# A TensorE loop for the products with V, and a fence that places the loads of the next step

## Chip, core and metric

The kernel runs on one core of a Trainium2 chip. The metric is the device time of one execution in microseconds (us), lower is better. The engines are PE (TensorE, with PEld for its weight loads), DVE (VectorE), ACT (ScalarE), POOL (GpSimd) and SP (SyncE, which here only issues DMAs). Each engine works through its own stream of instructions in order; engines wait for each other through semaphores.

## What is computed

One decode step of a transformer block: layer norm, attention of one query token per batch element over a cache of 8192 keys, output projection, and a gated MLP. What fills the time is the attention over the cache:

```python
B, Sq, D = 2, 1, 512
Hq, Hkv, Sk, Dh = 32, 32, 8192, 128          # k_cache, v_cache: (B, Hkv, Sk, Dh) in bf16
q = (layernorm(x) @ wq)                      # one row per batch element and head
scores = einsum("bhqd,bhkd->bhqk", q, k_cache) * Dh ** -0.5
p = softmax(scores)
o = einsum("bhqk,bhkd->bhqd", p, v_cache)
h = x + o.reshape(B, Sq, Hq * Dh) @ wo       # then a gated MLP of 512 x 1376
```

The two caches are 268 MB, each byte of which is used once.

## The kernel before

**Tiles and steps.** Four heads of one batch element make a step. Their keys are one tile of 8 MB (128 partitions x 32768 bf16), their values another. Fifteen whole steps (`steps[0]` to `steps[14]`, with `Q = LASTQ = 14`) and two half steps of two heads each cover all 64 heads. Three buffers of one tile each (`bufs`) are used in rotation in the order K0, V0, K1, V1, K2 and so on: V of step i+1 goes where K of step i was, K of step i+2 goes where V of step i was. So a load waits for the last reader of the tile that it replaces.

**One step** (the loop `for i in range(Q)` at the end of the kernel's attention part):

1. `scores_pe` (L343 to L370): PE transposes the last 24 of the 256 key columns of a partition (32 in step 0), ACT copies them back, PE multiplies them with the query.
2. `products` (L378) and `scores` (L396 to L402): DVE multiplies the other 232 columns with the query and adds them up by halving, about 33 us. This reads K for the last time.
3. `largest_of_own` and `place_own` (L413 to L423): DVE and ACT make the exponentials and lay them out as PE weights in `pgq`, with one group of 16 weight columns for each of 64 products.
4. `values` (L449): 64 products on PE, each a weight load of 128x16 and a matmul over 512 columns of V, all summed in one PSUM tile `pv_ps`. This reads V for the last time. Then ACT copies `pv_ps` to `pv` (L454).

In steps after 3, 7 and 11 the first eight products stand ahead of a small sum (`ahead = 8`).

**Order.** `tc.manual_schedule()` keeps every engine's instructions in the order in which the text issues them. Loads are issued by SP (`load_tile`, L168), in text order, each after its own waits. V of step i+1 is issued in the text after `scores` of step i and waits for DVE's last sum L398; K of step i+2 is issued after `values` of step i and waits for the last of its 64 products.

Of the kernel before, what the change touches and what calls it, by code (L numbers as in the profile page):

```python
# [7 lines left out]
ACT = mybir.ActivationFunctionType  # L8
# [15 lines left out]
def kernel(  # L24
# [13 lines left out]
    nc = tc.nc  # L38
    P = nc.NUM_PARTITIONS
    B, Sq, D = A_x.shape  # L40
    _, Hkv, Sk, Dh = A_k_cache.shape
# [13 lines left out]
    HALF = TILE // 2  # L55
    TPC = 8
    VG = 4


    NPE = 32  # L60
# [37 lines left out]
    qpair = consts.tile([P, 2, Dh], bf16)  # L98
    pgq = consts.tile([P, TILE // Dh // VG, NH, VG], bf16)
    pgp = consts.tile([P, 2, HALF // Dh // VG, 2, VG], bf16)  # L100
    pv = consts.tile([P, VG * Dh], f32)
    pick = consts.tile([P, VG, 4, NH], f32)
    zc = consts.tile([P, B, NQ, NH], f32)
# [56 lines left out]
    steps = [Step(i) for i in range(LASTQ + 3)]  # L160
    Q = LASTQ

    def load_tile(cache, s, dst, pieces=1):
        h = NH * s.g + (0 if s.quad else 2 * s.k)
        n = s.nt * Dh
        w = n // pieces
        for k in range(pieces):
            nc.sync.dma_start(  # L168
                out=dst[:, k * w:(k + 1) * w], in_=_dram(cache, (s.b * Hkv + h) * Sk * Dh + k * w, [[n, P], [1, w]]),
            )  # L170
# [16 lines left out]
        nc.vector.reciprocal(out=rstd, in_=rstd)  # L187
        nc.vector.tensor_tensor(out=dst_bkc, in0=dev, in1=_free(rstd, 0, [[1, B], [0, KC]]), op=ALU.mult)

    with tc.manual_schedule():  # L190

        for b, k, n in ((0, 0, KC), (1, 0, KC)):
            nc.scalar.dma_start(
                out=xr[b:b + 1, k * P:(k + n) * P], in_=_dram(A_x, b * D + k * P, [[D, 1], [1, n * P]]),
# [10 lines left out]
            out=nscale, in_=nscale, compare_op=ALU.not_equal, fill=-SCALE,  # L205
# [5 lines left out]
            out=ident_f, in_=ident_f, compare_op=ALU.not_equal, fill=1.0,  # L211
# [4 lines left out]
            out=sel, in_=sel, compare_op=ALU.not_equal, fill=1.0,  # L216
# [9 lines left out]
            out=pick, in_=pick, compare_op=ALU.not_equal, fill=1.0,  # L226
# [24 lines left out]
        for g0 in range(0, NQ, 4):  # L251
            for n0 in range(NH * g0 * Dh, NH * (g0 + 4) * Dh, 4 * Dh):
                q_ps = ps2.tile([B, 4 * Dh], f32, tag="o")
                for c in range(KC):
                    nc.tensor.matmul(  # L255
                        out=q_ps, lhsT=xn[:, c, :], rhs=wq_sb[:, c, n0:n0 + 4 * Dh], start=(c == 0), stop=(c == KC - 1),
                    )
                nc.vector.tensor_copy(qrow[:, n0:n0 + 4 * Dh], q_ps)  # L258
            for b in range(B):
                r_ps = ps2.tile([P, 4, Dh], f32, tag="tp")  # L260
                for j in range(NH):
                    nc.tensor.matmul(
                        out=r_ps[j * (P // NH):(j + 1) * (P // NH)], lhsT=sel[:, b, 0:P // NH],
                        rhs=_free(qrow, (NH * g0 + j) * Dh, [[NH * Dh, 4], [1, Dh]]), start=True, stop=True,
# [4 lines left out]
        for j in range(2):  # L269
            nc.tensor.matmul(  # L270
                out=r_ps[j * (P // 2):(j + 1) * (P // 2)], lhsT=sel[:, B - 1, :],
                rhs=_free(qrow, (Hq - NH + j) * Dh, [[2 * Dh, 2], [1, Dh]]), start=True, stop=True,
            )
        nc.scalar.activation(out=qpair, in_=r_ps, func=ACT.Copy)
        for b in range(B):
# [3 lines left out]
            nc.vector.tensor_copy(  # L279
                qTs[:, b].rearrange("p (g j) -> p g j", j=NH), _free(qT_ps, 0, [[P, NQ], [P // NH, NH]]),  # L280
            )
        load_tile(A_k_cache, steps[1], steps[1].kt)

        nc.gpsimd.tensor_copy(
            qzp[:, :, 6:8], qTs[:, B - 1, Hq - NH:Hq].rearrange("p (k j) -> p k j", j=2),
        )
# [42 lines left out]
        def scores_pe(s, between=lambda: None):  # L329


            U = s.npe // 4
            nh, nv = s.nh, s.nv
            row_ps = ps.tile([nh * U, 4 * P], f32, tag="row")

            def times_q(c0):
                for k in range(0, TPC, 4):
                    u = (c0 + k) // 4
                    if s.quad:
                        z = qz[:, QZ - NH - NH * u:QZ - NH - NH * u + NH * U]  # L340
                    else:
                        z = qzp[:, s.k, 6 - 2 * u:6 - 2 * u + 2 * U]
                    nc.tensor.matmul(  # L343
                        out=row_ps, lhsT=z, rhs=s.kt[:, (nv + c0 + k) * Dh:(nv + c0 + k + 4) * Dh],
                        start=(u == 0), stop=(u == U - 1),
                    )

            for c0 in range(0, s.npe, TPC):
                t_ps = ps2.tile([P, TPC, P], bf16, tag="tp")
                for k in range(TPC):  # L350
                    t = nv + c0 + k
                    nc.tensor.transpose(t_ps[:, k, :], s.kt[:, t * Dh:(t + 1) * Dh], ident)  # L352
                nc.scalar.activation(  # L353
                    out=s.kt[:, (nv + c0) * Dh:(nv + c0 + TPC) * Dh], in_=t_ps.rearrange("p t s -> p (t s)"), func=ACT.Copy,
                )
                between()
                if c0:
                    times_q(c0 - TPC)
            times_q(s.npe - TPC)
            rows = s.kt[0:nh * U, nv * Dh:nv * Dh + 8 * P].bitcast(f32)  # L360
            nc.scalar.activation(out=rows, in_=row_ps, func=ACT.Copy)  # L361
            between()
            sc_ps = ps.tile([P, 4, U, nh], f32, tag="row", name="sc_ps")
            for t in range(4):
                nc.tensor.transpose(  # L365
                    sc_ps[:, t].rearrange("p u j -> p (u j)"), rows[:, t * P:(t + 1) * P], ident_f[0:nh * U, 0:nh * U],
                )
            for j in range(nh):
                r = s.rows(j)
                nc.scalar.activation(  # L370
                    out=scols[s.i][r, nv:s.nt].rearrange("p (u t) -> p t u", t=4), in_=sc_ps[r, :, :, j], func=ACT.Copy,
                )
# [67 lines left out]

        pv_ps = {}

        def values(s, u0, u1):

            r = slice(32 * (s.g % 4), 32 * (s.g % 4) + s.nh * VG)
            if u0 == 0:
                pv_ps[s.i] = ps2.tile([P, VG * Dh], f32, tag="o", name="pv_ps")
            for u in range(u0, u1):
                nc.tensor.matmul(  # L449
                    out=pv_ps[s.i][r, :], lhsT=s.pg[:, u].rearrange("p j t -> p (j t)"),  # L450
                    rhs=s.vt[:, u * VG * Dh:(u + 1) * VG * Dh], start=(u == 0), stop=(u == s.nt // VG - 1),
                )
            if u1 == s.nt // VG:
                nc.scalar.activation(out=pv[r, :], in_=pv_ps[s.i][r, :], func=ACT.Copy)  # L454

        def diagonals(i):

# [54 lines left out]
        for i in range(Q):  # L512
            s = steps[i]
            scols[i] = small.tile([P, s.nt], f32, tag="scol", name="scol")
            scores_pe(s)
            place_q(steps[i + 1])
            products(s)
            if i - 2 in groups:
                shares(i - 2)
                normalise(i - 2)  # L520
            if i == Q - 1:
                lay_rows(0, [spread(0, b) for b in range(B)], scalar=True)
            scores(s)
            if i == Q - 2:
                load_tile(A_k_cache, steps[Q], steps[Q].kt)
            else:
                load_tile(A_v_cache, steps[i + 1], steps[i + 1].vt)
            if i == Q - 1:
                scores_pe(steps[Q])
            largest_of_own(s)  # L530
            if i == Q - 1:
                products(steps[Q], 0, NEXT)
            place_own(s)
            half = s.nt // VG // 2
            ahead = 8 if i - 1 in groups else 0
            if ahead:
                own_sums(i - 1)
                values(s, 0, ahead)
                sums(i - 1)
            values(s, ahead, half)  # L540
            if i == Q - 1:
                load_tile(A_k_cache, steps[Q + 1], steps[Q + 1].kt)
            values(s, half, 2 * half)
            if i in groups:
                diagonals(i)
            if i + 2 < Q:
                load_tile(A_k_cache, steps[i + 2], steps[i + 2].kt)
            elif i == Q - 2:
                load_tile(A_v_cache, steps[Q - 1], steps[Q - 1].vt)
            else:  # L550
                load_tile(A_k_cache, steps[Q + 2], steps[Q + 2].kt)


        s, p0, p1 = steps[Q:]
# [16 lines left out]
        at = [0, 0]  # L571
# [28 lines left out]
        turns = iter((first, second, third))  # L600
# [3 lines left out]
        for w, src in ((0, B_W_gate), (1, B_W_up)):  # L604
            nc.sync.dma_start(
                out=wgu[:, w].rearrange("p c f -> p (c f)"), in_=_dram(src, 0, [[KC * F, P], [1, KC * F]]),
# [4 lines left out]
        f0, n = FSETS[-2]  # L611
        for d0 in range(0, D, D // 2):
            nc.sync.dma_start(
                out=wd_sb[:, f0 // P:f0 // P + n, d0:d0 + D // 2],
                in_=_dram(B_W_down, f0 * D + d0, [[n * D, P], [D, n], [1, D // 2]]),
# [9 lines left out]
            out=z2_ps, lhsT=ones, rhs=_free(zc, ((B - 1) * NQ + groups[Q][1]) * NH, [[1, nb]]), start=True, stop=True,  # L625
# [11 lines left out]
            out=parts3, in0=ident[0:PARTS, HI:HI + B], in1=ident[0:PARTS, LOW:LOW + B], op=ALU.add,  # L637
# [3 lines left out]
        half = p1.nt // 2  # L641
# [53 lines left out]
        for c in range(KC):  # L695
            nc.tensor.transpose(hT_ps[:, c, :], hb[:, c], ident)
        nc.scalar.activation(
            out=hrow.rearrange("q (p c) -> q p c", c=KC), in_=hT_ps.rearrange("q c p -> q p c"), func=ACT.Copy,
# [3 lines left out]
            out=shift, in0=_free(g_ps, ONE, [[ONE + 1, FC], [0, B]]), in1=_free(mean, 0, [[0, FC], [1, B]]), op=ALU.mult,  # L702
# [3 lines left out]
            out=gate, in_=_free(g_ps, 0, [[ONE + 1, FC], [1, B], [B, 2]]), axis=AXIS.X, op=ALU.add,  # L706
# [7 lines left out]
            out=gate, in0=gate, scalar=0.0, in1=_free(rvar, 0, [[0, FC], [1, B]]), op0=ALU.max, op1=ALU.mult,  # L714
# [63 lines left out]
```

## Time and profile before

| | |
|---|---|
| median of 3 runs | 659.2 us (659.19 to 659.33) |
| the profiled execution | 658.71 us, span 656.9 us |
| DVE busy | 557.1 us (85% of the span) |
| PE busy | 348.8 us (53%), granted clock 0.761 on average |
| ACT busy | 123.6 us (19%) |
| HBM read | 281.09 MB, 428 GB/s over the span |
| products with V (PE L449) | 960 of 128x512, 239.7 us busy |

"Span" is the time from the first to the last instruction in the trace; what the execution's own time has above it (1.8 us) lies around it. Busy shares are shares of the span. The chain of waits in such a profile is followed back from the last instruction: at each step to what released it.

### The profile page before, as it was taken

Reading aid. Unit: us, or ns where it says so; the run is one execution under the profiler, and the core shown is the slowest. Engines: PE = TensorE matmul, PEld = TensorE weight load, DVE = VectorE, ACT = ScalarE, POOL = GpSimd, SP = SyncE. Lnnn points to the kernel's source line nnn. Section 1 sums busy time; section 2 is a strip of 40 time slices with the busy share of each in tenths; the row PEclk is TensorE's granted clock in tenths of the full one; section 3 lists DMA queues with packets and bytes.
Section 4 is the critical chain, followed back from the end, with each engine's and each line's share of the span. In section 5 each row is a group of like instructions: output and inputs, shape, how many; then the busy total and the mean of one; then the engine's idle time right before and its main releaser. Section 6 shows DMA issues by size and latency. Waiting matters only on the chain.

```text
span 656.9 us, 5097 instructions
## 1 busy us (share of the span) xinstructions
PE 348.8 (53%) x2116; PEld 157.9 (24%) x2116; DVE 557.1 (85%) x248; ACT 123.6 (19%) x337; POOL 9.1 (1%) x37
## 2 busy tenths in 40 slices
PE   2530924709175380926538092562909458291997
PEld 1210311304022130312214031220403224130456
DVE  1399697988979799897979989797997969999982
ACT  1130030300203030030302103030210304201870
POOL 3000000000000000000000000000000000000020
PEclk9875876958778695877959588695957869576895
DMA  9999999999999999999999999999999999999997
GB/s 383 447 444 443 391 448 439 447 443 397 447 439 432 447 408 447 431 435 436 423 447 424 435 440 427 443 420 439 443 423 440 419 448 435 423 440 408 430 428 296
DMA packets 6766, 281.40 MB, mean 428 GB/s; under 512 B 724, under 2 KB 1368, under 8 KB 1624
## 3 DMA queue, kind: packets, MB, share of 16 engines
q1 hardware_dynamic: 6740, 281.09, 99.1%
q8 instruction: 16, 0.26, 0.1%
q14 instruction: 6, 0.05, 0.0%
q10 hardware_dynamic: 4, 0.00, 0.0%
HBM read 281.09 MB, written 0.00 MB: 428 GB/s over the span
## 4 chain that ended last, share of the span: by engine, by line
DVE 42%; DMA 40%; PE 16%; ACT 1%; issue 1%; SPq 0%; DVEq 0%; ACTq 0%
DMA tile<-in_A_k_cache_dram 31%; DVE tile L378 19%; DVE tile L396 18%; PE pv_ps L449 15%; DMA tile<-in_B_W_down_dram 4%; DMA tile<-in_A_wo_dram 4%; DVE scol L398 2%; DMA tile<-in_A_wq_dram 2%; PE q_ps L255 2%; DVE pgq L423 1%; ACT ecol L418 1%; DVE pm L402 0%; DVE qrep L398 0%; DVE pm L413 0%; DVE hmax L415 0%
## 5 line engine op out<-in xcount | busy, mean ns | idle before, releaser
L449 PE MATMUL pv_ps<-tile,pgq 128*16 128x512 bf16 x960 | 239.7, 415 | 239.9 <-DVE pgq L423 227.8
L378 DVE TENSOR_TENSOR tile<-tile,qrep 128x29696 bf16<-128x29696 bf16 (+3 forms) x16 | 232.4, 14524 | 49.0 <-DMA tile<-in_A_k_cache_dram 49.0
L396 DVE TENSOR_TENSOR tile<-tile 128x14848 bf16<-128x14848 bf16 (+7 forms) x68 | 236.4, 3477 | 2.2
L449 PEld LDWEIGHTS <-pgq 128*16 128x16 bf16 x960 | 90.7, 96 | 378.6 <-DVE pgq L423 238.5
L353 ACT ACTIVATE tile<-t_ps 128x1024 bf16<-128x1024 bf16 x53 | 52.6, 1022 | 17.4 <-PE t_ps L352 16.9
L454 ACT ACTIVATE pv<-pv_ps 16x512 f32<-16x512 f32 (+1 forms) x16 | 9.4, 588 | 238.9 <-PE pv_ps L449 238.8
L418 ACT ACTIVATE ecol<-scol,nmax 128x256 bf16<-128x256 f32 x14 | 7.1, 508 | 200.1 <-DVE nmax L417 200.1
L352 PE MATMUL t_ps<-ident,tile 128*128 128x128 bf16 x424 | 32.0, 227 | 17.5 <-DMA tile<-in_A_k_cache_dram 17.5
L343 PE MATMUL row_ps<-tile,qz 128*24 128x512 bf16 (+1 forms) x98 | 30.9, 398 | 17.9 <-ACT tile L353 17.8
L352 PEld LDWEIGHTS <-tile 128*128 128x128 bf16 x424 | 25.4, 102 | 32.7 <-DMA tile<-in_A_k_cache_dram 18.2
L398 DVE TENSOR_REDUCE scol<-tile 128x232 f32<-128x1856 bf16 (+1 forms) x14 | 28.9, 2067 | 0.5
L423 DVE TENSOR_TENSOR pgq<-ecol,ownb 128x1024 bf16<-128x1024 bf16 x15 | 10.4, 691 | 10.3 <-ACT ecol L418 10.3
L384 ACT ACTIVATE tile<-tile 128x128 bf16<-128x128 bf16 x60 | 17.6, 294 | 1.9 <-DVE tile L378 1.9
L378 DVE TENSOR_TENSOR tile<-tile,qpair 128x4096 bf16<-128x4096 bf16 (+3 forms) x4 | 15.5, 3881 | 0.0
L343 PEld LDWEIGHTS <-qz 128*24 128x24 bf16 (+1 forms) x98 | 7.9, 92 | 27.8 <-issue 22.7
L365 PE MATMUL sc_ps<-ident_f,tile 24*128 24x24 f32 (+2 forms) x68 | 7.4, 224 | 11.0 <-ACT tile L361 11.0
L370 ACT ACTIVATE scol<-sc_ps 32x24 f32<-32x24 f32 (+1 forms) x56 | 11.7, 209 | 7.7 <-PE sc_ps L365 7.2
L361 ACT ACTIVATE tile<-row_ps 24x512 f32<-24x512 f32 (+2 forms) x17 | 9.9, 585 | 14.0 <-PE row_ps L343 14.0
L258 DVE CAST tile<-q_ps 2x512 bf16<-2x512 f32 x8 | 5.4, 679 | 7.2 <-PE q_ps L255 7.2
L255 PE MATMUL q_ps<-tile,xn 128*2 128x512 bf16 x32 | 10.0, 477 | 2.5 <-DMA tile<-in_A_wq_dram 2.5
L384 ACT ACTIVATION_READ_ACCUMULATOR tile<-tile 128x1 f32 x60 | 11.2, 187 | 0.0
L365 PEld LDWEIGHTS sc_ps<-ident_f,tile 24*128 24x128 f32 (+2 forms) x68 | 5.6, 141 | 19.8 <-ACT tile L361 19.8
(135 smaller groups left out, 124.9 us busy)
## 6 DMA issues: line engine op xcount, KB each, us to landing
tile<-in_A_k_cache_dram SPq DMA_DIRECT2D x2, 4096.0 KB, 19.1
tile<-in_A_v_cache_dram SPq DMA_DIRECT2D x2, 4096.0 KB, 20.5
tile<-in_A_wq_dram SPq DMA_DIRECT2D x1, 4096.0 KB, 12.2
tile<-in_A_wo_dram SPq DMA_DIRECT2D x1, 2048.0 KB, 24.1
tile<-in_A_wo_dram SPq DMA_DIRECT2D x2, 1024.0 KB, 23.4
tile<-in_B_W_gate_dram SPq DMA_DIRECT2D x1, 1376.0 KB
tile<-in_B_W_up_dram SPq DMA_DIRECT2D x1, 1376.0 KB, 26.8
tile<-in_B_W_down_dram SPq DMA_DIRECT2D x1, 640.0 KB, 27.7
```

Source lines behind the costliest of these rows:

```text
L255: nc.tensor.matmul(out=q_ps, lhsT=xn[:, c, :], rhs=wq_sb[:, c, n0:n0 + 4 * Dh], start=(c == 0), stop=(c == KC - 1),)
L343: nc.tensor.matmul(out=row_ps, lhsT=z, rhs=s.kt[:, (nv + c0 + k) * Dh:(nv + c0 + k + 4) * Dh], start=(u == 0), stop=(u == U - 1),)
L352: nc.tensor.transpose(t_ps[:, k, :], s.kt[:, t * Dh:(t + 1) * Dh], ident)
L353: nc.scalar.activation(out=s.kt[:, (nv + c0) * Dh:(nv + c0 + TPC) * Dh], in_=t_ps.rearrange("p t s -> p (t s)"), func=ACT.Copy,)
L365: nc.tensor.transpose(sc_ps[:, t].rearrange("p u j -> p (u j)"), rows[:, t * P:(t + 1) * P], ident_f[0:nh * U, 0:nh * U],)
L378: nc.vector.tensor_tensor(out=kv, in0=kv, in1=_free(s.qr, 0, [[0, n], [1, Dh]]), op=ALU.mult)
L384: nc.scalar.activation(out=kv, in_=kv, func=ACT.Copy, accum_out=scols[s.i][:, t:t + 1])
L396: nc.vector.tensor_tensor(out=lo, in0=lo, in1=hi, op=ALU.add)
L398: nc.vector.tensor_reduce(out=scol[:, s.na:s.nv], in_=_free(s.kt, s.na * Dh, [[Dh, s.nv - s.na], [1, 8]]), axis=AXIS.X, op=ALU.add,)
L418: nc.scalar.activation(out=ecol, in_=scols[s.i], func=ACT.Exp, scale=SCALE, bias=nmax, accum_out=zs[:, s.b, s.g:s.g + 1],)
L423: nc.vector.tensor_tensor(out=s.pg, in0=_free(ecol, 0, [[VG, s.nt // VG], [0, NH], [1, VG]]), in1=_free(ownb, 0, [[0, s.nt // VG], [VG, NH ...
L449: nc.tensor.matmul(out=pv_ps[s.i][r, :], lhsT=s.pg[:, u].rearrange("p j t -> p (j t)"), rhs=s.vt[:, u * VG * Dh:(u + 1) * VG * Dh], start= ...
```

## The change

In steps 0 to 12 the 64 products with V are written as a few single products, a loop on TensorE with four products per turn, and one last single product. The single ones in front number three, so that 60 remain for 15 turns (52 for 13 turns in the steps with `ahead = 8`). Inside the loop the addresses of the weights and of V come from a register that steps by 64; the built program has in one turn four fused register instructions (each with five or six register operations), four matmuls with register addresses, one register addition and one compare-and-branch. The loop stands in `tc.tile_critical()`, which puts it into a block of its own: all engines' programs get an unconditional branch there, and PE gets semaphore waits, a no-op and a drain around the loop.

The loads of step i+1 stand in the text behind that loop, with `tc.no_sync_barrier()` between. In the built program SP's sequence of loads is the one it was, and each load waits for the same last reader as before, apart from the loop's exit, which now stands for the end of the products. Step 13 and the half steps keep their single products. The scheduler is told to keep the written order on PE, DVE, ACT and SP, so POOL's instructions are placed by the scheduler. The products now always write partitions 0 to 15 of `pv_ps`, and ACT's copy moves them to their place in `pv`.

```diff
+    VU = 4
...
-    with tc.manual_schedule():
+    with tc.manual_schedule(engines={mybir.EngineType.PE, mybir.EngineType.DVE, mybir.EngineType.Activation, mybir.EngineType.SP}):
...
-        load_tile(A_k_cache, steps[1], steps[1].kt)
-
...
-        def values(s, u0, u1):
+        def values(s, u0, u1, looped=False):
...
+            n = s.nh * VG
...
+            out = pv_ps[s.i][0:n, :]
+            w = s.pg.rearrange("p u j t -> p (u j t)")
+
+            def step(u):
                 nc.tensor.matmul(
-                    out=pv_ps[s.i][r, :], lhsT=s.pg[:, u].rearrange("p j t -> p (j t)"),
-                    rhs=s.vt[:, u * VG * Dh:(u + 1) * VG * Dh], start=(u == 0), stop=(u == s.nt // VG - 1),
+                    out=out, lhsT=w[:, u * n:(u + 1) * n], rhs=s.vt[:, u * VG * Dh:(u + 1) * VG * Dh],
+                    start=(u == 0), stop=(u == s.nt // VG - 1),
                 )
+
+            def turns(u, v):
+                with tc.tile_critical(), nc.tensor.Fori(u * n, (v - VU) * n + 1, VU * n) as at:
+                    for k in range(VU):
+                        nc.tensor.matmul(
+                            out=out, lhsT=w[:, bass.ds(at + k * n, n)],
+                            rhs=s.vt[:, bass.ds(at * (VG * Dh // n) + k * VG * Dh, VG * Dh)],
+                            start=False, stop=False, skip_group_check=True,
+                        )
+
+            if looped:
+                lead = (s.nt // VG - 1 - max(u0, 1)) % VU + max(u0, 1)
+                for u in range(u0, lead):
+                    step(u)
+                turns(lead, s.nt // VG - 1)
+                step(s.nt // VG - 1)
...
             scores(s)
-            if i == Q - 2:
-                load_tile(A_k_cache, steps[Q], steps[Q].kt)
-            else:
-                load_tile(A_v_cache, steps[i + 1], steps[i + 1].vt)
...
+            if i < Q - 1:
+                values(s, ahead, whole, looped=True)
+                tc.no_sync_barrier()
+                load_tile(A_k_cache, steps[i + 1], steps[i + 1].kt)
+                if i < Q - 2:
+                    load_tile(A_v_cache, steps[i + 1], steps[i + 1].vt)
+                else:
+                    load_tile(A_k_cache, steps[Q], steps[Q].kt)
+                    load_tile(A_v_cache, steps[Q - 1], steps[Q - 1].vt)
```

More of the change, by code (lines that the diff above doesn't have):

```diff
@@ L441 @@
         pv_ps = {}
-        def values(s, u0, u1):
+        def values(s, u0, u1, looped=False):
             r = slice(32 * (s.g % 4), 32 * (s.g % 4) + s.nh * VG)
+            n = s.nh * VG
             if u0 == 0:
                 pv_ps[s.i] = ps2.tile([P, VG * Dh], f32, tag="o", name="pv_ps")
-            for u in range(u0, u1):
+            out = pv_ps[s.i][0:n, :]
+            w = s.pg.rearrange("p u j t -> p (u j t)")
+            def step(u):
                 nc.tensor.matmul(
-                    out=pv_ps[s.i][r, :], lhsT=s.pg[:, u].rearrange("p j t -> p (j t)"),
-                    rhs=s.vt[:, u * VG * Dh:(u + 1) * VG * Dh], start=(u == 0), stop=(u == s.nt // VG - 1),
-                )
+                    out=out, lhsT=w[:, u * n:(u + 1) * n], rhs=s.vt[:, u * VG * Dh:(u + 1) * VG * Dh],
+                    start=(u == 0), stop=(u == s.nt // VG - 1),
+                )
+            def turns(u, v):
[13 more added lines that the diff above has]
+            else:
+                for u in range(u0, u1):
+                    step(u)
             if u1 == s.nt // VG:
-                nc.scalar.activation(out=pv[r, :], in_=pv_ps[s.i][r, :], func=ACT.Copy)
+                nc.scalar.activation(out=pv[r, :], in_=out, func=ACT.Copy)
         def diagonals(i):
@@ L523 @@
             scores(s)
-            if i == Q - 2:
-                load_tile(A_k_cache, steps[Q], steps[Q].kt)
-            else:
-                load_tile(A_v_cache, steps[i + 1], steps[i + 1].vt)
             if i == Q - 1:
+                load_tile(A_v_cache, steps[Q], steps[Q].vt)
                 scores_pe(steps[Q])
@@ L533 @@
             place_own(s)
-            half = s.nt // VG // 2
+            whole = s.nt // VG
+            half = whole // 2
             ahead = 8 if i - 1 in groups else 0
@@ L539 @@
                 sums(i - 1)
-            values(s, ahead, half)
-            if i == Q - 1:
+            if i < Q - 1:
[4 more added lines that the diff above has]
+                    load_tile(A_v_cache, steps[i + 1], steps[i + 1].vt)
+                else:
+                    load_tile(A_k_cache, steps[Q], steps[Q].kt)
+                    load_tile(A_v_cache, steps[Q - 1], steps[Q - 1].vt)
+            else:
+                values(s, ahead, half)
                 load_tile(A_k_cache, steps[Q + 1], steps[Q + 1].kt)
-            values(s, half, 2 * half)
+                values(s, half, whole)
+                load_tile(A_k_cache, steps[Q + 2], steps[Q + 2].kt)
             if i in groups:
                 diagonals(i)
[L546 to L551, printed above, removed]
         s, p0, p1 = steps[Q:]
```

## The prediction, made before the changed kernel ran

> **What bounds the kernel now.** I read the DMA queues first, then the chain of waits in order of time, then the waits, and last the rows that can price the new instructions.
>
> ```profile
> q1 hardware_dynamic: 6740, 281.09, 99.1%
> q8 instruction: 16, 0.26, 0.1%
> ```
>
> The data queue keeps all 16 DMA engines busy for 99.1% of the span, so the stream of tiles sets the time. Only a gap in that stream, or less of it, changes the time by much. The chain shows where a gap could open:
>
> ```profile
> 107.72 15.38 PE pv_ps L449 x64
> 123.11 26.45 DMA tile<-in_A_k_cache_dram
> 149.59 15.64 DVE tile L378
> ...
> 185.25 15.86 PE pv_ps L449 x64
> 201.13 25.73 DMA tile<-in_A_k_cache_dram
> 226.89 15.62 DVE tile L378
> ...
> 262.80 16.33 PE pv_ps L449 x64
> 279.15 24.98 DMA tile<-in_A_k_cache_dram
> 304.15 15.64 DVE tile L378
> ```
>
> Columns are start, duration, what. A K tile is issued the moment the 64 products end, and DVE starts the moment it lands. From 149.59 to 304.15 eight tiles pass, 19.3 us each. But the loads last 26.45, 25.73 and 24.98 us (later rows of the chain: 26.45, 26.37, 26.41): the rest is time in line behind V of the step between. So K is issued early by 7.1, 6.4, 5.7, 7.1, 7.1 and 7.1 us, 6.8 on average. The first load was issued at 0.73, and the trace's DMA records have its first packet at 1.77; less this 1.04 us, the products may end **5.7 us later** on average (4.6 at the tightest) before the DMA engines run dry. The start-up could count up to 2.5 us (the first half tile took 12.19 us in the chain, against 9.65 at stream speed), which would leave 4.3.
>
> ```profile
> DVE tile L378 <- DMA tile<-in_A_k_cache_dram: 49.0, 14, 5.2
> ```
>
> DVE waits 49.0 us in 14 waits for K, 3.5 us a step: it has slack of its own.
>
> **What a later end of the products costs.** Let D be how much later they end, per step. Up to 5.7 us nothing. Beyond it the chain K, DVE, products, K two steps on is longer than four tiles, and the DMA stream loses the excess once in two steps (a late K of an even step gives the odd step's K the same relief). Thirteen loops are 6.5 such pairs: cost = 6.5 x (D - 5.7).
>
> **The loop's turn.** Four products now take this long on PE (weight loads, one per product):
>
> ```profile
> 188.20 0.14 PEld L449 LDWEIGHTS <-pgq 128*16 128x16 bf16 x1 [0.29 <-issue]
> 188.63 0.14 PEld L449 LDWEIGHTS <-pgq 128*16 128x16 bf16 x1 [0.29 <-issue]
> 189.05 11.54 PEld L449 LDWEIGHTS <-pgq 128*16 128x16 bf16 x54 [0.29 <-issue]
> ```
>
> The pitch is 0.427 us for the first nine (granted clock 0.5) and 11.54/54 = 0.214 after that: 1.71 us per turn for about two turns, then 0.855. A loop whose sequencer work fits in 0.855 us costs nothing. Before has no register instruction or branch on PE; the nearest rows are:
>
> ```profile
> L773 PEldq EVENT_SEMAPHORE  x2: 51/51/51, 656.4 to 656.9; - x2
> L773 PEldq DRAIN  x2: 13/230/448, 654.2 to 656.6; - x2
> L225 POOLq MOVE  x1: 29/29/29, 2.7 to 2.7; - x1
> 634.41 2.29 PE L505 MATMUL att_ps<-orow,tile 128*128 128x2 bf16 x64
> ```
>
> - A fused register instruction holds five or six operations: at least one control instruction of PE, 51 ns, at most six, 306. I take 6 x 29 = 174 by the only register row, the move.
> - A weight load and matmul with register addresses: at least the 2.29/64 = 36 ns of a pair with plain addresses, at most that and two control instructions, 138. I take two control instructions, 102, since a register has to be read for each.
> - The addition: 51. The taken branch: at least 51; at most a fetch of code anew, 930 (the 16 packets of q8 carry the PE program, 4,097 instructions in 0.26 MB, and the DMA records have 880 to 971 ns for each). I take three control instructions, 153 (compare, jump, first read). [...]
>
> One turn: 4 x (174 + 102) + 51 + 153 = **1.31 us**; the ends are 0.45 and 2.76. Against 0.855 that is 13 x 0.453 = 5.9 us, less 2 x 0.4 gained while the clock is half and the sequencer is ahead: 5.1 us.
>
> **The loop's ends.** PE's entry waits for its own lead products (0.17 us of drain: a record of 0.379 less 0.214), then passes eight or nine semaphore waits, a no-op, two branches and a move (13 x 51 = 0.66), and the first addresses (0.28): 1.1. The exit drains (0.17), passes a drain (row: 13 to 448 ns, taken 230) and about four control instructions (0.2): 0.6. Together 1.7 us, from 1.0 to 3. The waits themselves end at once: they ask for V of this step, the exponentials, and loads that DVE has already used; no load of the next step is among them. Behind the waiting PE stand only the products and then `scores_pe` of the next step, which ends at 128.8 where DVE needs it at 144.1 (15 us of cover).
>
> D = 5.1 + 1.7 = **6.8 us**; cost 6.5 x (6.8 - 5.7) = +7.2 us.
>
> **What else moves.** SP's order of loads and their waits are the same, so the moved text costs nothing by itself: K and V of step i+1 wait for the same readers, and SP's branches fall in its idle time. The branches on DVE (13 x 51 ns at most) lie in the 3.5 us per step that it waits for K, those on ACT in its idle 81%. POOL, busy for 9.1 us, waits 602.8 us in one stretch. ACT's copy keeps its 0.59 us. What goes: 756 written products, for 52 in loops. PE's program falls from 4,097 to some 2,970 instructions, 16 to 12 fetches of 16 KB, each 0.93 us on one of 16 DMA engines. In the DMA records the engines end between 649.6 and 653.1, those with fetches last, each with two at most; four fetches fewer save nothing up to 1.9 us. I take -0.5, since only the last engine counts.
>
> Sum: 658.7 + 7.2 - 0.5 = 665.4 for an execution like the profiled one, whose 658.71 is 0.5 under the median of 659.2: **666 us**.
>
> **Rivals.**
>
> *The turn fits, and the loop is hidden.* If the turn is 1.16 us or less, D is 13 x (1.16 - 0.855) - 2 x 0.55 + 1.7 = 4.6 us, the tightest K's slack, and the stream never breaks. What is left is -0.5: 658.7 us. For it: the 0.45 us bound, and that I priced every register operation singly though they come fused in one instruction. Against it: it needs either fused instructions of about 137 ns or a pair at about 65.
>
> *The clock stays at half, or the turn takes near 2 us.* A PE that waits for its sequencer a third of the time might not be granted full speed. Then a turn is 1.71 us, D is 13 x 0.855 + 1.7 = 12.8, the cost 6.5 x 7.1 = 46, the time 705. Against it:
>
> ```profile
> 108.00:112.00 4.00, 4.00 (x14) 1.46 (x13) 1.02 (x1) 0.00 (x0) 0.00 (x0) 0.68 1.17 508
> ...
> 124.00:128.00 4.00, 2.35 (x16) 0.92 (x14) 3.97 (x2) 2.94 (x4) 0.00 (x0) 1.00 0.68 295
> ```
>
> Columns: stretch, length, busy time and count of PE, PEld, DVE, ACT and POOL, granted clock, DMA share, GB/s. The clock rises within some 4 us of work, and stays at 1.00 over 4 us in which PE is busy for 2.35 (59%); my loop keeps it busy 0.855/1.31 = 65%.
>
> *Code is fetched anew.* A loop that lies across the border of two 16 KB blocks of PE's code might fetch at every turn. A fetch takes 0.93 us behind a packet of up to 2.42 on its engine. One such loop would lose 15 x 0.93 = 14 to 15 x 3.35 = 50 us, once, less the 5.7 of slack: 666 + 8 to 666 + 44, middle 690. About 14 instructions of a loop in 256 of a block, 13 times, make 0.7 such loops likely. Against it: no PE idle time in before's products goes with its fetches, so blocks are there ahead, and the one left behind is probably kept. [...]
>
> *Faster.* Only the fetches could do it: 1.9 us at most, 657.3, if the last DMA engine is one that loses two, and the loop is hidden.
>
> *The fence fails,* and a loop's entry waits for the next tiles: V of the next step lands 22.6 us after the products start (130.3 in the DMA records against 107.7), which would add that to D and cost 6.5 x (22.6 - 5.7) = 110 us or more. The built order has no such wait, so it gets no chance of its own.
>
> **From the cases to the numbers.** Forecast case (turn 1.16 to 1.6 us; 659.5 to 690): 0.43. Hidden (within 0.2%): 0.37. Half clock or a turn near 2 us: 0.09. Fetches: 0.06. Faster by over 0.2%: 0.05. A difference of 0.2% (1.3 us) is about what a measurement of this kernel can tell from no change. So slower 0.58, same 0.37, faster 0.05. The range must take in the hidden case with what fetches may save, 657.8, and above most of the forecast case's costs: 13 x 0.745 - 0.2 + 1.7 = 11.2 at a turn of 1.6 us costs 36 us, 694; I end it at 700, which leaves out part of the half clock, half of the fetches' upper end, and turns over 1.65 us, together with the low side under 0.2. Where the forecast case alone holds, its range is 659.5 to 690.
>
> **What would show it.** In the changed kernel's trace: the span from `pgq` to the last product, 15.4 to 16.4 us now, should be some 22; matmuls inside a warm turn come at 0.3 us or more apart with PE sequencer rows of 0.1 to 0.3 us between, and clock 1.00. K issues should come at or after the landing of V before them, DVE's waits for K should grow from 49.0 to about 56 us, and the DMA queue's share fall to about 98%. If the products end within 20 us, the hidden case holds and DVE's waits stay near 49. A product stretch of 28 us at clock 0.5 is the third case; one single stretch of over 30 is the fetch case; q8 should have 12 packets, and more would say that loops fetch. I am wrong about the path if K is issued late and the DMA share stays at 99.1%, and about the price if the turn differs from 1.31 us.

## The result, and the profile after

The changed kernel takes 667.56 us in the median (666.47 to 669.34) beside 659.2 for the kernel before: a ratio of 1.0131, 95% interval [1.0108, 1.0154]. The profiled execution took 667.86 us, 665.7 of it span, so 8.8 us of span are to be found. The total is 1.6 us from the prediction, but two of its terms were wrong, in opposite directions.

The lines of the changed kernel's page that answer to those shown of before (span; queue, packets, MB, share of the 16 DMA engines; DVE's multiplication of K with busy time, mean ns, idle time ahead of it):

```profile
span 665.7 us, 6427 instructions
q1 hardware_dynamic: 6740, 281.09, 98.6%
q8 instruction: 11, 0.18, 0.1%
L377 DVE TENSOR_TENSOR tile<-tile,qrep 128x29696 bf16<-128x29696 bf16 (+3 forms) x16 | 232.4, 14524 | 57.4 <-DMA tile<-in_A_k_cache_dram 57.4
```

The same bytes take longer, the DMA share falls from 99.1 to 98.6%, and DVE's waits for K grow from 49.0 to 57.4 us, 8.4 more. The loss is in the stream of tiles. In the DMA records it can be added up: over the 16 engines, mean idle time inside the stream of K and V grew from 0.01 to 3.1 us, and the 64 KB packets, 2.418 us each at stream speed, took 6.3 us per engine above that speed instead of 0.6. That is 3.1 + 5.7 = 8.8 us. By landings it comes out much the same: V of step 14 landed 8.3 us later (603.68, before 595.35), and 0.4 us came after it. **More was lost to slow packets than to idle engines.**

The products of step 1 on PE (timeline: start, length, what, count, idle time before and its releaser; 107.72, 15.37 long and in one row, before):

```profile
107.98 1.45 PE L452 MATMUL pv_ps<-tile,pgq 128*16 128x512 bf16 x3 [16.56 <-DVE pgq L422]
110.67 15.48 PE L460 MATMUL pv_ps<-tile,pgq 128*16 x60 [1.24 <-issue]
126.34 0.38 PE L452 MATMUL pv_ps<-tile,pgq 128*16 128x512 bf16 x1 [0.20 <-PEq L458]
```

The 60 products of the loop take 15.48 us, hardly more than 60 plain ones; the pauses at the entry (1.24) and the exit (0.20) are new. Over steps 0 to 12 the first and last product start 18.60 us apart on average, 15.55 before: **D is 3.05 us, not 6.8.** The loads of K, on SP (the prediction's "issued early" is the time from here to the landing of V in line ahead):

```profile
302.51 0.33 SPq L169 DMA_DIRECT2D tile<-in_A_v_cache_dram  x1
324.26 0.33 SPq L169 DMA_DIRECT2D tile<-in_A_k_cache_dram  x1
341.15 0.33 SPq L169 DMA_DIRECT2D tile<-in_A_v_cache_dram  x1
362.35 0.33 SPq L169 DMA_DIRECT2D tile<-in_A_k_cache_dram  x1
```

V landed at 327.30 by the DMA records, so the K load of 324.26 was still 3.0 us ahead; yet K landed 21.43 us after V, where a tile at stream speed needs 8 x 2.418 = 19.34. Six of the eleven loads K2 to K12 were 2.85 to 3.9 us ahead; before, none was under 5.6.

What a turn costs is in the rows by source line (engine, operation, count, ns min/median/max, first and last start):

```profile
L458 PEldq FUSED_REGOPS  x189: 78/78/83, 69.5 to 559.2; - x189
L458 PEldq ALU_OP  x189: 36/36/39, 70.2 to 559.8; - x189
L458 PEldq COMPARE_BRANCH  x189: 76/208/226, 70.3 to 559.9; - x189
L460 PEldq FUSED_REGOPS  x567: 74/74/74, 69.7 to 559.7; - x189
```

Four fused instructions start 0.153 us apart with a pair between them, the addition takes 36 ns and a taken branch 208 (76 when it falls through). A turn is 0.98 to 1.02 us in the sequencer.

### The profile page after: what moved, and what is told of

It reads as the page before. It is cut to its first block, busy times and chain, and to the rows that moved or that the text cites. A ratio compares the mean times of both kernels' runs of the same rounds, so it can differ in the third digit from the quotient of the medians.

```text
span 665.7 us, 6427 instructions
## 1 busy us (share of the span) xinstructions
PE 368.2 (55%) x2116; PEld 158.9 (24%) x2116; DVE 557.1 (84%) x248; ACT 123.5 (19%) x337; POOL 9.0 (1%) x37
## 3 DMA queue, kind: packets, MB, share of 16 engines
q1 hardware_dynamic: 6740, 281.09, 98.6%
## 5 line engine op out<-in xcount | busy, mean ns | idle before, releaser
L377 DVE TENSOR_TENSOR tile<-tile,qrep 128x29696 bf16<-128x29696 bf16 (+3 forms) x16 | 232.4, 14524 | 57.4 <-DMA tile<-in_A_k_cache_dram 57.4
L460 PE MATMUL pv_ps<-tile,pgq 128*16 x756 | 193.7, 415 | 16.5 <-issue 8.8
L452 PE MATMUL pv_ps<-tile,pgq 128*16 128x512 bf16 x204 | 65.5, 468 | 210.9 <-DVE pgq L422 198.1
L460 PEld LDWEIGHTS pv_ps<-tile,pgq 128*16 x756 | 71.9, 95 | 142.7 <-issue 76.7
L452 PEld LDWEIGHTS <-pgq 128*16 128x16 bf16 x204 | 18.9, 100 | 245.6 <-DVE pgq L422 206.2
```

The source lines that it names most:

```text
L377: nc.vector.tensor_tensor(out=kv, in0=kv, in1=_free(s.qr, 0, [[0, n], [1, Dh]]), op=ALU.mult)
L452: nc.tensor.matmul(out=out, lhsT=w[:, u * n:(u + 1) * n], rhs=s.vt[:, u * VG * Dh:(u + 1) * VG * Dh], start=(u == 0), stop=(u == s.nt // V ...
L460: nc.tensor.matmul(out=out, lhsT=w[:, bass.ds(at + k * n, n)], rhs=s.vt[:, bass.ds(at * (VG * Dh // n) + k * VG * Dh, VG * Dh)], start=Fal ...
```

## The experiments

My theory after the result: products that end later cost time even while K is still issued ahead of the landing of V, by slow packets as well as by idle engines, and nothing else in the change costs anything. Rivals: the moved loads, POOL's new order or the branches cost something by themselves; or the loop disturbs PE in some way that the end of the products does not show. All times are medians; "kernel 1" is the kernel of experiment 1; the kernel before took 658.77 to 658.81 beside these runs.

**1. The change without its loop.** The loads, the fence and POOL's order stay.

```diff
-                values(s, ahead, whole, looped=True)
+                values(s, ahead, whole)
```

> The changed text with its fence, its place of the loads and its schedule, but all 64 products written out, no loop. Theory A (the time is lost only because the products end later, so that K is issued too shortly before the DMA engines run dry): back to the kernel before, 659.2 within 0.7 us, products of 15 to 16.5 us. Rival B (the moved loads, the fence or POOL's freed order cost the time): stays near 667. Rival C (the loop's blocks cost, by the branches on all engines, apart from lateness): also 659, so this run tells only A and C from B.

Measured: 659.0 us, ratio 1.0003 [0.9994, 1.0013]. From this kernel's page:

```profile
span 657.3 us, 5096 instructions
q1 hardware_dynamic: 6740, 281.09, 99.1%
q8 instruction: 16, 0.26, 0.1%
```

The moved loads, the fence and POOL's order are free; all the loss comes with the loop. This kernel has the sixteen fetches of code of the kernel before, so it does not test the prediction's -0.5 for fewer of them; no run here shows such a gain.

**2. Late products without a loop.** Kernel 1, with products whose weights are zero added ahead of the last product of steps 0 to 12: they add zeros to the sum, and take 0.21 us each.

```diff
+                    if u == s.nt // VG - 1 and s.i < Q - 1:
+                        for _ in range(LATER):
+                            nc.tensor.matmul(
+                                out=out, lhsT=qz[:, QZ:QZ + n], rhs=s.vt[:, 0:VG * Dh],
+                                start=False, stop=False,
+                            )
```

With 14 of them:

> As e1_unrolled, and in steps 0 to 12 fourteen more matmuls with zero weights before the last product: no loop, but the products end 14 x 0.214 = 3.0 us later, as much as they do with the loop (18.6 against 15.6 us from first to last start). Theory A: 667 (665 to 669), DMA gaps at the same K tiles. Rival C: lateness of 3 us lies within the slack of 5.7 us that the prediction took, so 659 to 660.

With 7:

> As e2_late14 with seven zero-weight matmuls, so the products end 1.5 us later than written out. K would then be issued about 5 us ahead of the landing of the V before it, 3.8 at the tightest. Theory A with the deadline that the traces show (trouble under about 4 us): 659 to 660.5, a gap or two. A cost in proportion to lateness from zero on (9 us for 3 us) would give 663.5.

With 28:

> As e2_late14 with 28 zero-weight matmuls, 6.0 us later. Theory A: 3 us more than e2 in 13 steps, at one loss per two steps 6.5 x 3 = 19 us above e2: 687 (683 to 692). The prediction's slack of 5.7 us: 659 + 6.5 x 0.3 = 661 (that slack already fell with e2; the run measures the slope).

Measured: 662.0 us with 7 (ratio 1.0048 [1.0033, 1.0063]), 667.97 with 14 (1.0146 [1.0126, 1.0166]), 678.66 with 28 (1.0309 [1.0293, 1.0324]). The timeline of step 1 with 14 shows what was done:

```profile
108.19 15.92 PE L453 MATMUL pv_ps<-tile,pgq 128*16 128x512 bf16 x63 [16.25 <-DVE pgq L423]
123.94 3.18 PE L477 MATMUL pv_ps<-tile,qz 128*16 128x512 bf16 x14
126.96 0.38 PE L453 MATMUL pv_ps<-tile,pgq 128*16 128x512 bf16 x1
```

The last product starts at 126.96 there and at 126.34 in the changed kernel. K2 to K12 (K of steps 2 to 12) were issued 4.26 us ahead of the landing of V on average, in the changed kernel 4.31, before 6.72. A plain program that is as late as the loop costs as much as the loop: the cause is the lateness. The expectations for 7 and 28 were both missed, and show the law wrong at both ends:

| added | first to last start, us | above kernel 1 | cost above kernel 1 | 6.5 x (D - 5.7) |
|---|---|---|---|---|
| 7 | 17.25 | 1.4 | 3.0 | 0 |
| 14 | 18.70 | 2.8 | 9.0 | 0 |
| 28 | 21.73 | 5.9 | 19.7 | 1 |

The loss is there at 1.4 us and then grows by 3.5 to 4 us per us, not 6.5. (Of the 3.0 us with 7, the stream of the profiled execution shows 1.6: V of step 14 landed at 597.46, in kernel 1 at 595.83.) Why: the 14 profiled executions of this study hold 154 loads K2 to K12. Sorted by how long before the landing of the V ahead of it a K was issued, this is how long after that V it landed:

| issued ahead, us | loads | landed after V, us (mean) | packets above 2.418 us, per engine |
|---|---|---|---|
| under 2 | 7 | 21.3 | 0.7 |
| 2 to 4 | 31 | 20.3 | 0.6 |
| 4 to 4.5 | 14 | 19.8 | 0.4 |
| 4.5 to 5 | 15 | 19.4 | 0.1 |
| over 5 | 87 | 19.35 | 0.03 |

**The edge lies at about 4.5 us ahead, not at 1.04.** Below it a load loses about 1 us on average, some half of it in slow packets. The DMA records show two parts of this edge:

- The landing of a tile is the end of its last DMA engine: each tile has 16 landing records, those of the V ahead of the K load of 324.26 from 325.03 to 327.30. In the kernel before, the first engine was through with V 2.2 us ahead of the landing on average (1.8 to 3.0), in the changed kernel 2.6. That engine needs K's packets then, not at the landing.
- A load's first packet came about as early as at the start of the kernel (in the changed kernel 0.98 and 0.97 us after the issue: 324.26 to 325.24, 404.25 to 405.22; 1.04 at the start), but such early packets were slow. Over the 154 loads, first packets of an engine that started within 1.3 us of the issue took 3.14 us on average (257 packets, none under 2.6), those 2 to 3 us after it 2.61, and those from 4 us on 2.43.

That the loss is no more than 3.5 to 4 per us has a visible reason too: a K that lands late gives the next K, whose products did not wait for it, its lead back (with 28 added: 0.35 us ahead, then 4.03, 1.30, 2.24, 0.42, 4.25).

**3. Longer turns.** `VU` 4 becomes 12, so five or four turns per step.

```diff
-    VU = 4
+    VU = 12
```

> The changed kernel with 12 products per turn (5 turns, 4 in the steps with ahead), so a turn's sequencer work of about 12 x 0.15 + 0.4 = 2.3 us fits under 12 x 0.214 = 2.57. Theory A with the prices of the trace (the turn of four, 1.02 us, was hidden by the cold start in ten steps and cost about 1.5 us in steps 4, 8 and 12 alone): 664 to 666.5. The prediction's price (the turn's excess is 5.1 us of each step's lateness): the lateness falls to under 2 us, 659 to 660.

Measured: 665.11 us, ratio 1.0092 [1.0076, 1.0109], as forecast from the trace's prices. First to last start is 18.06 us, 0.54 less than with turns of four, for 2.4 us: the turns are only a small part of D. Steps 4, 8 and 12 make two thirds of it, about 1.5 us each. In the changed kernel the sequencer was up to 2.1 us ahead of the matmuls in step 1, but 0.13 us in step 4, where the first eight products stand ahead of a small sum.

**4. Longer turns and 15 products ahead of the loop,** so that the pause at the entry falls after the clock has risen.

```diff
-                lead = (s.nt // VG - 1 - max(u0, 1)) % VU + max(u0, 1)
+                lead = 15
```

> As e3_turns_of_12, with 15 single products ahead of the loop (48 in 4 turns), so that TensorE's clock has risen before the pause at the loop's entry. Theory A with the clock as a part of the lateness (about four more products at half clock, 0.8 us): the lateness falls to entry 1.4 + exit 0.4 = 1.8 us, 659.5 to 661.5, with 8 or 9 products at a pitch of 0.427 as in the kernel before. If the clock has no part, the lateness stays near 3 and the time near that of e3.

Measured: 662.82 us, ratio 1.0074 [1.0053, 1.0096]; first to last start 17.61 us. That is over the forecast of 659.5 to 661.5: 2.06 us of D are left, not 1.8. Step 1 in this experiment:

```profile
107.80 5.07 PE L452 MATMUL pv_ps<-tile,pgq 128*16 128x512 bf16 x15 [17.91 <-DVE pgq L422]
114.11 10.52 PE L460 MATMUL pv_ps<-tile,pgq 128*16 x48 [1.24 <-issue]
```

The pause is as long as in the changed kernel, but the clock has risen by then: the 15 products ahead of it take 5.07 us, where 15 at the half-clock pitch of 0.427 would take 6.4. The windows of step 1 (columns as in the prediction), first one of the kernel before (its 108 to 112, at 0.68, is in the prediction), then the changed kernel's:

```profile
112.00:116.00 4.00, 4.00 (x20) 1.62 (x19) 4.00 (x1) 0.00 (x0) 0.00 (x0) 1.00 0.72 311
...
108.00:112.00 4.00, 2.76 (x7) 0.76 (x8) 1.17 (x1) 0.00 (x0) 0.00 (x0) 0.50 1.17 508
112.00:116.00 4.00, 4.00 (x12) 1.32 (x11) 4.00 (x1) 0.00 (x0) 0.00 (x0) 0.56 0.64 279
116.00:120.00 4.00, 4.00 (x21) 1.68 (x19) 4.00 (x1) 0.00 (x0) 0.00 (x0) 1.00 1.18 508
```

In the changed kernel the pause (109.43 to 110.67) falls where the clock rose before: by the clock records it rose at 115.50, before at 110.56. On average 11.9 starts of a step lie a half-clock pitch apart, against 8.2 before: 3.6 x 0.213 = 0.8 us of D. But in this experiment it is 9.9, and 9.9 in kernel 1 too, which has no loop. So 0.4 us go with the pause; why kernel 1 has 0.4 us more than the kernel before is not shown. The rise came 2.8 us after the first product before, and 7.5 us after it with a pause behind three products.

**5. Without the fence.** The loads go back to their places in the text of before; the loop stays as changed.

```diff
-                tc.no_sync_barrier()
-                load_tile(A_k_cache, steps[i + 1], steps[i + 1].kt)
...
+                    load_tile(A_k_cache, steps[i + 2], steps[i + 2].kt)
```

> The changed kernel without the fence, the loads at their old places in the text (K of step 1 ahead of the loop over the steps, V of step i+1 after the scores, K of step i+2 after the products). In its built order a loop's entry waits also for K of the next step; V of the next step stands behind the loop. K lands 3 to 4 us after the products begin, the entry is reached after about 1.9, so the lateness grows by 1 to 2.5 us. Theory A at 6.5 us per us: 674 to 684. If the entry's wait has no effect: 667.

Measured: 674.9 us in two executions, ratio 1.0244 [1.0223, 1.0265]. Steps 1 and 2 on PE:

```profile
108.24 1.45 PE L453 MATMUL pv_ps<-tile,pgq 128*16 128x512 bf16 x3 [13.18 <-DVE pgq L423]
111.89 15.13 PE L461 MATMUL pv_ps<-tile,pgq 128*16 x60 [2.20 <-DMA tile<-in_A_k_cache_dram]
...
146.95 1.45 PE L453 MATMUL pv_ps<-tile,pgq 128*16 128x512 bf16 x3 [13.63 <-DVE pgq L423]
152.43 15.34 PE L461 MATMUL pv_ps<-tile,pgq 128*16 x60 [4.03 <-issue]
```

The entry of the loop now waits for the next K, 2.20 us in step 1. In step 2 the releaser is not told, but K landed at 151.26, and in 11 of the 13 steps the loop started 0.6 to 1.2 us after the next K's landing. All eleven loads K2 to K12 fall under the edge. So the fence does what it says, and saves 7 of the 16 us that the loop alone would cost.

**6. Room for a late end.** Experiment 4 with 32 instead of 24 key columns on TensorE in steps 1 to 10: DVE's multiplication falls from 15.63 to 15.09 us and its additions likewise, so the products start earlier.

```diff
-    NPE_AT = {**{i: 24 for i in range(1, 11)}, LASTQ: 24, LASTQ + 1: 16, LASTQ + 2: 16}
+    NPE_AT = {**{i: 32 for i in range(1, 11)}, LASTQ: 24, LASTQ + 1: 16, LASTQ + 2: 16}
```

> e4_lead_15 with 32 instead of 24 key columns given to PE in steps 1 to 10: DVE has 8 of 232 columns less, 1.1 us per step, so the products start and end 1.1 us earlier and K is issued about 5.6 us early again. Theory A: nothing is lost any more, 658 to 659, with five fetches of code fewer than before. Rival C (the loop's blocks cost by themselves): 661.5 to 663 as e4.

Measured: 660.41 us, ratio 1.0025 [1.0016, 1.0034], between the two forecasts. The stream is whole again (idle 0.01 us, slow packets 0.8; V of step 13 landed at 576.07, before at 576.06), though the products are as long as in experiment 4 (17.52 us). The 1.6 us that are left therefore lie behind the stream. The same edit to the changed kernel itself, turns of four:

> The changed kernel as it is, four products a turn, with 32 columns on TensorE in steps 1 to 10 only. VectorE's multiplication of K falls from 15.63 to 15.09 us and its additions by a similar share, so weights and products start some 1.2 us earlier in ten steps. If the cost is lateness of the products against the loads' turn, as the kernels with added products say (0.2 us at none, 3.2 at 1.5 us, 9.2 at 3 us): lateness falls from 3.05 to some 1.8 us, which gives 662 to 664.5 us. If what costs is the loop itself (its fences, its code): 666 to 668.5 us.

Measured: 664.32 us, ratio 1.0083 [1.0067, 1.01], as the lateness has it: the loop is as long as in the changed kernel (18.74 us from first to last start against 18.60), and only because it starts earlier, the time falls by 3.2 us. The columns without any loop:

> No loop, 32 columns on TensorE in steps 1 to 10 as in the kernel with 15 single products ahead. Tells what the 32 columns do by themselves. If the stream of transfers bounds the kernel and the loads were early enough already, nothing is to be had: 658.5 to 659.2 us. If the earlier hand-over is itself worth time: under 658.3 us. If the extra transposes and copies cost: over 659.3 us, and then part of the 1.6 us left is theirs and not the loop's.

Measured: 659.49 us, ratio 1.0008 [1.0000, 1.0017]. An earlier start is worth nothing where the loads were early enough; about 0.7 of the 1.6 us left in experiment 6 is there without a loop as well. Here too the stream is whole (V of step 14 landed at 595.95, in kernel 1 at 595.83).

**7. What is left: the end of the kernel.** From the landing of V of step 14 to the end of the span, experiment 6 takes 63.15 us, kernel 1 61.48 and the kernel before 61.58. PE's last matmuls of W_down have a pause in experiment 6 (last two lines) that before does not have (first two):

```profile
652.23 0.27 PE L728 MATMUL d_ps<-tile 7*2 7x128 bf16 x4
652.55 0.81 PE L728 MATMUL d_ps<-tile,hm 128*2 128x128 bf16 x24
...
652.71 0.27 PE L752 MATMUL d_ps<-tile 7*2 7x128 bf16 x4
654.46 1.34 PE L752 MATMUL d_ps<-tile,hm 128*2 128x128 bf16 x44 [1.49 <-issue]
```

Another of 0.59 us lies 256 instructions ahead of it (at 348 and 92 instructions from the end of PE's program), and a packet of q8 started 2.34 and 2.40 us ahead of the resumptions. The changed kernel itself has two such pauses, of 0.42 and 0.63 us. I moved the code by transposes of the identity ahead of those of the keys in steps 0 to 6:

```diff
+                for k in range(4 if s.i < 7 else 0 if c0 == 0 else 0):
+                    nc.tensor.transpose(t_ps[:, k % TPC, :], ident, ident)
```

> The kernel with turns of twelve, 15 single products ahead and 32 columns on TensorE, plus four transposes of the identity ahead of the first transposes in each of steps 0 to 6 (28 pairs of instructions, into a tile that is overwritten before it is read). Counted from the end of TensorE's program the pauses of 0.76 and 1.75 us of the last kernel lay at 348 and 92, 256 apart; 56 more instructions ahead move such borders to 404 and 148, where the kernel before has its own without a visible pause. Theory that the remaining 1.6 us is code that comes too late at these borders: 658.6 to 659.4 us, and the two pauses are gone or lie at 404 and 148. Rival, that the loop's turns or exits cost it: 660.0 to 660.8 us, pauses as they were.

The edit does more than that text says: it stands in each of four groups of columns, so it added 112 pairs (224 instructions), not 28. Measured: 660.67 us, ratio 1.0022 [1.0012, 1.0032], the time of the rival, though the pauses did not stay as they were. They are now:

```profile
646.55 0.53 PE L529 MATMUL att_ps<-orow,tile 128*128 128x2 bf16 x12 [0.62 <-issue]
...
652.45 0.59 PE L754 MATMUL d_ps<-tile,hm 128*2 128x128 bf16 x16
653.97 0.92 PE L754 MATMUL d_ps<-tile,hm 128*2 128x128 bf16 x28 [0.93 <-issue]
```

They lie at 316 and 60 from the end: 92 + 224 = 316, and 256 further on 60. The pauses are tied to the place in the code; the edit moved them to other points of the dense runs of small matmuls, so the time without them was not measured. The span of the profiled execution did get shorter (657.6 us, experiment 6: 658.5), but 2.8 us lay outside it instead of 2.1; why is open. The counterpart, kernel 1 with 101 such transposes:

> No loop, 24 columns, plus 101 transposes of the identity in steps 0 to 12 (eight a step, five in the last), which moves a border of 256 instructions from 146 to 92 ahead of the end of TensorE's program, in the last dense run of small matmuls. If late code at a border costs a straight program as well: a pause of 1 to 2 us 92 instructions before the end and 660 to 661 us. If the late code is only met behind loops: 658.8 to 659.4 us and no pause there.

Measured: 659.41 us, ratio 1.0009 [1.0000, 1.0018]. No pause at 92, since I had the border wrong: I had counted from the program's length. But there is one, at 411:

```profile
644.10 0.37 PE L529 MATMUL att_ps<-orow,tile 128*128 128x2 bf16 x7
645.58 0.73 PE L529 MATMUL att_ps<-orow,tile 128*128 128x2 bf16 x17 [1.11 <-issue]
```

This kernel has 202 instructions of PE more than kernel 1. The one with 32 columns and no loop has 200 more, and its pause (1.37 us) lies two nearer to the end, at 409. So a straight program meets such borders too; in kernel 1 the same count puts them at 209 and 465, where no pause shows. Where a pause shows at one, PE is idle for 0.42 (the changed kernel) to 1.49 us (experiment 6), in a dense run of small matmuls (44 in 1.34 us in experiment 6).

## Why the prediction was right or wrong, step by step

- **The stream of tiles bounds it, and a late end of the products is the price:** right, shown by experiments 1, 2 and 6. DMA share (98.6 for "about 98%"), DVE's waits (57.4 for "about 56 us") and the fetches (11 for 12) came as written. But K was to be issued at or after the landing of V ahead of it; it was still 2.85 us or more ahead.
- **"The products may end 5.7 us later":** wrong, and the worst step. The 1.04 us between issue and first packet held, but it was taken off a lead that was measured to the landing of V, the end of the last DMA engine. The first engine was free 2.2 us earlier, and packets that started soon after the issue were slow (3.14 us within 1.3 us of it, against 2.418), so loss set in at about 4.5 us ahead. Of the average lead of 6.7 us about 2 were free, and less for the tighter loads.
- **"6.5 x (D - 5.7)":** wrong with it. It gives nothing at the measured D of 3.05. The cost has no sharp edge, since the loads' leads differ, and grows by 3.5 to 4 per us.
- **"One turn: 1.31 us", 5.1 us per step:** wrong in size. The fused instruction was taken at 174 ns and takes 74 to 78; the pair was 102 and is under 80; the branch was 153 and takes 208. The turn is 1.0 instead of 1.31. And the cover at half clock is larger than the two turns at 0.4 that I took: the sequencer ran some 2 us ahead, enough for thirteen turns at 0.15 too long, so in ten steps the turns cost little. Steps 4, 8 and 12 alone make 0.35 us of D over all steps.
- **Entry 1.1 and exit 0.6:** short by 0.3 us in sum. From the start of one product to the start of the next, the entry adds 1.84 - 0.21 = 1.6 us and the exit 0.57 - 0.21 = 0.4.
- **The clock:** missing. I priced the pause at the entry, not that it comes while the clock is still low; in step 1 the clock then rose at 115.50 us, before at 110.56. Products at half clock add 0.8 us, of which 0.4 us are in kernel 1 too and so are not the pause's. So D is 1.6 + 0.4 + 0.8 + 0.35 = 3.1.
- **Rivals:** by its own price, 4.6 us of slack, the hidden case should have held with this D; it failed on that slack. Its sign came (products within 20 us), and DVE's waits grew all the same. By the clock records the half clock held for 6.6 us of a step's products on average (3.8 before), not for all of the loop. No loop fetched its code anew (11 packets). The fence holds (experiment 5).

So +7.2 was forecast from a D too large by 3.75 us and a slack too large by about as much, and +8.4 came out. The mechanism stands; that the number fits is mostly chance, since the two errors cancelled.

What stays open: why packets that start soon after their load's issue are slow; and what the loop would cost in experiment 6 without the two pauses at its end. Next to the kernel with the same columns and no loop it is 0.9 us, which the pauses could make up, but this is not shown. No version here was faster than the kernel before.

## What to carry to other kernels

The slack of a load was not its lead over the landing ahead of it less the time to a first packet: the first engine was through with V 2.2 us ahead of its landing on average before and 2.6 in the changed kernel, and a late load's first packets were slow (3.14 us instead of 2.418). Look in the trace for how far ahead the tightest load is issued, and how its landing moves when that shrinks, before trading that lead away. The loop here cost its entry and exit (2.0 us a step), and what the pause did to the clock (0.4), more than its turns (0.35); put the entry where the clock is already up (experiment 4: 17.61 us from first to last start instead of 18.06), and give the time back elsewhere on the same path. When two terms of a sum are guessed, test each one alone: here a loop whose lateness was made up (32 columns) and lateness without a loop (zero products) told what the total could not.

## What the runs showed of the hardware that was not expected

- Over the 154 loads K2 to K12, a K that was issued 2 to 4 us ahead of the landing of the V before it landed 20.3 us after that V on average, one issued 4.5 to 5 us ahead 19.4, one issued over 5 us ahead 19.35. First packets that started within 1.3 us of the issue took 3.14 us instead of 2.418.
- In PE's sequencer a fused register instruction of the changed kernel took 74 to 78 ns, an addition 36, a compare-and-branch 208 taken and 76 not taken.
- With a pause of 1.24 us after three products the granted clock in step 1 rose at 115.50 us, without it at 110.56.
- At points 256 instructions apart (348 and 92 from the end of PE's program in experiment 6, 316 and 60 with the code moved) PE stood idle for 0.59 to 1.49 us in dense runs of small matmuls. It went on 2.3 to 2.4 us after the start of a 16 KB packet of q8 (2.38 and 2.32 in the changed kernel, 2.34 and 2.40 in experiment 6); that packet itself took 0.88 and 0.93 in the changed kernel.
